# Seven block products in place of eight in the second layer of a fused attention and two-layer kernel

## The chip, the cores and the metric

The kernel runs on one core of a Trainium2 chip. The core has TensorE (PE in the profile; PEld is its loading of weights), VectorE (DVE), ScalarE (ACT), GpSimd (POOL) and SyncE (SP), which run side by side, each through its own instructions in a fixed order, and wait for each other at semaphores. PE reads SBUF and writes PSUM. The metric is the time of one execution on the device in microseconds (us), as the median of several runs.

## The reference

Attention with a mask by hashes is followed by two layers on 1536 tokens. The change touches the second layer alone (`_moe2_ref`), which has 512 inputs, 1536 hidden features and 512 outputs:

```python
def _moe2_ref(x, w_gate, w_val, w_out):
    gate = 1.0 / (1.0 + np.exp(-(x @ w_gate)))
    val = x @ w_val
    return (gate * val @ w_out).astype(np.float32)
```

## The kernel before

All products are made in three terms: an operand is split into a high part (rounded to the type fp32r, by ScalarE) and a low part (source minus high part, by GpSimd or VectorE), and `three` adds high x high, low x high and high x low into one PSUM tile. A 512-row contraction is thus 4 (`kc`) x 3 matmuls.

The tokens are cut into three sweeps of 512 (`CH`). In the second layer a sweep runs over 12 f-tiles of 128 hidden features. `tiles` lists all (layer, sweep, f-tile) in order; the last 24 entries are the second and the third sweep of the second layer, f-tiles 0 to 11 twice. For each tile the loop in `moe` does the following:

- `weights` splits the tile's piece of w_gate and of w_val (`wah`, `wal`, `wbh`, `wbl`; low parts on GpSimd, line 699).
- `stage1` makes the two first products, gate into the PSUM tile `pa`, value into `pb`, 12 matmuls of 512 token columns each.
- `post` takes the sigmoid of `pa` (ScalarE, `a`), multiplies it into `pb` (VectorE, line 745) and splits that into `gh` (ScalarE) and `gl` (VectorE, line 748).
- `second`, one tile behind, multiplies `gh` and `gl` with the split piece of w_out (`wth`, and `wtl` by VectorE at line 699) and adds into four PSUM tiles `m0` to `m3`, 12 matmuls of 512 columns. After the last f-tile of a sweep the four are copied out and stored.

The raw weights come from memory as 64-bit numbers and are decoded (`decode`) into SBUF, where all of them stay; decoding ends in the first sweep of the second layer. In this last stage the order on each engine is set by a list scheduler that works from its own estimates of durations; the source gives it priorities by the place in the program.

Of the kernel before, what the change touches and what calls it, by code (L numbers as in the profile page):

```python
# [229 lines left out]
def lsh_attention_moe_moe2_kernel(  # L230
# [380 lines left out]
    def open_mw():  # L611
        mw = Tiles(ctx.enter_context(tc.tile_pool(name="mw", bufs=1, side="left", reuse_waits="tile")), "mw", 1)
        late["mw"] = mw
        for nm in ("w1", "w2"):
            late[nm] = [mw.tile([P, KC, P], F32, name=f"{nm}r{i}") for i in range(NF1)]
        late["xh"] = mw.tile([P, KC, CH], F32R, name="xh")
        late["xl"] = mw.tile([P, KC, CH], F32R, name="xl")
# [102 lines left out]
    def moe(psM):  # L720


        tiles = [(1, s, fi) for s in range(1, NSW) for fi in range(NF1)] + [(2, s, fi) for s in range(NSW) for fi in range(NF2)]
        mp, mw = late["mp"], late["mw"]
        x2 = [(late["xh"], late["xl"])]
        x2 += [[mp.tile([P, KC, CH], F32R, name=f"x2_{i}_{t}") for i in range(2)] for t in range(1, NSW)]
        split_x(1, x2[1], range(KC))

        def weights(n):

            if n >= len(tiles):
                return None
            m, s, fi = tiles[n]
            ga, gb = (late["w1"][fi], late["w2"][fi]) if m == 1 else ftile(fi)[:2]
            return [split_w(mp, "wa", ga), split_w(mp, "wb", gb)]

        def post(n, ps):
            m, s, fi = tiles[n]
            a = mp.tile([P, CH], F32, tag="a", name="a", bufs=2)
            if m == 1:  # L740
                act_copy(a, ps[0])
            else:
                act.activation(out=a, in_=ps[0], func=AF.Sigmoid)
# [7 lines left out]
        def second(n, g, wt, acc):  # L751
            m, s, fi = tiles[n]
            nf = NF1 if m == 1 else NF2
            last = n == len(tiles) - 1
            mm = None
            for c in range(4):
                cs = slice(c * P, (c + 1) * P)
                with tc.issue_after(mm.ins) if last and c else nullcontext():
                    if m == 1:
                        mm = three(acc[c], [t[:, cs] for t in wt], g, fi == 0, fi == nf - 1)  # L760
                    else:
                        mm = three(acc[c], [t[:, cs] for t in g], wt, fi == 0, fi == nf - 1)
            if fi < nf - 1:
                return
            for c in range(4):
                if m == 1:
                    act_copy(x2[s][0][:, c], acc[c])
                    dve.tensor_tensor(out=x2[s][1][:, c], in0=acc[c], in1=f(x2[s][0][:, c]), op=ALU.subtract)
                else:
                    o = mp.tile([P, DM], F32, tag="a" if last and c < 2 else "o", name="o", bufs=2)  # L770
                    if last and c % 2:
                        dve.tensor_copy(o, acc[c])
                    else:
                        act_copy(o, acc[c])
                    b, n = divmod(s * (CH // P) + c, NT)
                    sync.dma_start(out=out[b * S:(b + 1) * S].rearrange("(p c) d -> c p d", c=NT)[n], in_=o)

        ops = {0: weights(0), 1: weights(1)}
        gs, wts = {}, {}
        acc = None  # L780
        for n in range(len(tiles) + 1):
            if n < len(tiles):
                ps = [psM.tile([P, 512], F32, tag=t, name=t) for t in ("pa", "pb")]
                x = x2[tiles[n][1]]
                w = ops.pop(n)
                for kcs in ([range(KC)] if n else [range(KC - 1), range(KC - 1, KC)]):
                    for i in range(2):
                        stage1(ps[i], w[i], x, kcs)
                m, s, fi = tiles[n]
                wts[n] = split_w(mp, "wt", wc[:, fi] if m == 1 else ftile(fi)[2], eng=dve)  # L790
                gs[n] = post(n, ps)
# [5 lines left out]
            second(n - 1, gs.pop(n - 1), wts.pop(n - 1), acc)  # L797
# [3 lines left out]
            if n + 1 < len(tiles):  # L801
                ops[n + 1] = weights(n + 1)
            if n == 3:
                split_x(2, x2[2], range(KC))

    def decodes(n):

# [127 lines left out]
```

## Time and profile before

| | |
|---|---|
| median of 3 runs | 826.63 us (825.66 to 826.91) |
| profiled execution | 824.83 us |
| its span, first to last instruction | 823.0 us |
| PE busy | 795.7 us, 97% of the span |
| DVE, ACT, POOL busy | 523.7, 511.1, 347.6 us |
| mean granted clock of PE | 1.00 |

The span is what the rows are measured in; the execution's own time has 1.8 us around it. A row of the trace names the engine, the line of the kernel, the operation and its tiles (out<-in). The duration of an instruction reaches from its start to its modelled end, and the next of the same engine can start before that.

### The profile page before, as it was taken

The page shows a single profiled execution, that of the slowest core. Times are in us where ns is not written, and L with a number is a line of the kernel's source. Part 1 is how long each engine was busy: PE and PEld are TensorE (multiplying, and loading weights), DVE is VectorE, ACT ScalarE, POOL GpSimd, SP SyncE. Part 2 cuts the span into 40 slices and gives each one's busy share as a digit, 9 for nine tenths or more (in the row PEclk, how much of TensorE's full clock was granted, in tenths as well). Part 3 has the DMA queues.
Part 4 walks back from the last instruction along what each step waited for, and adds up shares of the span by engine and source line. Part 5 has one row for each costly group of instructions (what it writes and reads, how often), then busy time and mean ns, then how long its engine had stood idle before and what let it go on. Part 6 is the DMA issues. An engine that isn't in the chain of part 4 may idle for free.

```text
span 823.0 us, 11970 instructions
## 1 busy us (share of the span) xinstructions
PE 795.7 (97%) x4144; PEld 667.9 (81%) x4144; DVE 523.7 (64%) x929; ACT 511.1 (62%) x993; POOL 347.6 (42%) x360
## 2 busy tenths in 40 slices
PE   6898999999999999999999999999999999999998
PEld 4676888888788888888888888888888888888886
DVE  7869989888799989988175545686642222322222
ACT  6888878776788888777355555755634333343332
POOL 4566443133565464349333434444533333333330
PEclk9999999999999999999999999999999999999999
DMA  7865645344354544330013122343301000010001
GB/s 234 211 200 171 187 115 158 98 122 122 96 155 132 148 129 115 101 111 13 1 53 101 53 77 77 103 129 127 103 1 52 0 1 1 0 52 1 0 1 52
DMA packets 45949, 74.11 MB, mean 90 GB/s; under 512 B 6336, under 2 KB 32960, under 8 KB 45888
## 3 DMA queue, kind: packets, MB, share of 16 engines
q1 hardware_dynamic: 45888, 73.34, 30.5%
q8 instruction: 33, 0.54, 0.3%
q14 instruction: 28, 0.23, 0.1%
HBM read 52.43 MB, written 3.19 MB: 68 GB/s over the span
## 4 chain that ended last, share of the span: by engine, by line
PE 83%; DVE 9%; ACT 2%; DMA 2%; POOL 2%; issue 1%; SPq 0%; POOLq 0%; DVEq 0%; ACTq 0%
PE pa L705 17%; PE m L705 17%; PE pb L705 17%; PE av L541 7%; PE tp L523 5%; PE wacc L600 4%; PE p L705 4%; PE s L469 3%; PE s L472 3%; DVE s L479 3%; PE y L705 2%; PE gps L402 2%; DVE pt L528 2%; DVE da L338 1%; PE trr L394 1%
## 5 line engine op out<-in xcount | busy, mean ns | idle before, releaser
L745 DVE TENSOR_TENSOR pb<-pb,a 128x512 f32<-128x512 f32 x52 | 36.3, 698 | 147.7 <-PE pb L705 140.4
L523 PE MATMUL tp<-idf,e 128*128 128x128 f32 x576 | 102.4, 275 | 5.8 <-DVE pt L528 5.4
L490 ACT ACTIVATE e<-s,sm 128x768 f32<-128x768 f32 x96 | 95.8, 1000 | 15.7 <-DVE sm L480 14.9
L526 ACT ACTIVATE pt<-tp 128x384 fp32r<-128x384 f32 (+1 forms) x192 | 89.9, 493 | 19.8 <-PE tp L523 17.4
L705 PE MATMUL pa<-x,wah 128*128 128x512 f32 x320 | 98.7, 389 | 0.0
L336 POOL TENSOR_SCALAR da<-da 128x512 f32<-128x512 f32 x76 | 52.7, 695 | 108.9 <-ACT da L334 104.4
L479 DVE TENSOR_REDUCE s<-s 128x1 f32<-128x768 f32 x96 | 91.1, 954 | 11.6 <-PE s L472 10.4
L705 PE MATMUL pb<-x,wbh 128*128 128x512 f32 x320 | 98.5, 389 | 0.0
L699 POOL TENSOR_TENSOR wal<-xall,wah 128x512 fp32r<-128x512 f32 x36 | 47.4, 1316 | 110.1 <-ACT wah L277 109.6
L528 DVE TENSOR_TENSOR pt<-tp,pt 128x384 fp32r<-128x384 f32 x168 | 87.8, 547 | 4.1 <-ACT pt L526 2.9
L523 PEld LDWEIGHTS tp<-idf,e 128*128 128x128 f32 x576 | 71.3, 140 | 19.6 <-DVE pt L528 6.8
L541 PE MATMUL av<-pt,spv 128*128 128x256 f32 (+1 forms) x576 | 85.1, 297 | 1.7 <-DVE pt L528 1.4
L541 PEld LDWEIGHTS av<-pt,spv 128*128 128x128 f32 (+1 forms) x576 | 72.6, 182 | 11.1 <-DVE pt L528 2.4
L334 ACT ACTIVATE da<-st 128x512 f32<-128x512 f32 x76 | 51.0, 671 | 48.6 <-DVE w1r L343 20.6
L705 PEld LDWEIGHTS pb<-x,wbh 128*128 128x128 f32 x320 | 60.1, 188 | 12.5
L705 PEld LDWEIGHTS pa<-x,wah 128*128 128x128 f32 x320 | 60.1, 188 | 12.5
L469 PE MATMUL s<-bk,bq 128*128 128x384 f32 x192 | 61.9, 384 | 6.3 <-ACT e L490 6.0
L600 PE MATMUL wacc<-wo,t 128*128 128x512 f32 x192 | 64.1, 416 | 1.7 <-DVE pt L528 1.6
L705 PE MATMUL pb<-x,wbl 128*128 128x512 f32 x160 | 62.3, 389 | 0.0
L705 PE MATMUL pa<-x,wal 128*128 128x512 f32 x160 | 62.2, 390 | 0.0
L748 DVE TENSOR_TENSOR gl<-pb,gh 128x512 fp32r<-128x512 f32 x52 | 35.9, 690 | 39.8 <-ACT gh L277 39.8
L338 DVE SCALAR_TENSOR_TENSOR da<-st,da 128x512 uint32<-128x512 uint32 x76 | 58.5, 771 | 1.2
(143 smaller groups left out, 1856.6 us busy)
## 6 DMA issues: line engine op xcount, KB each, us to landing
st<-in_moe_w_dram SPq DMA_DIRECT2D x32, 512.0 KB, 4.1
st<-in_moe_w_out_dram SPq DMA_DIRECT2D x20, 512.0 KB, 3.7
st<-in_moe_w_gate_dram SPq DMA_DIRECT2D x12, 512.0 KB, 3.5
st<-in_moe_w_val_dram SPq DMA_DIRECT2D x12, 512.0 KB, 3.5
rawq<-in_q_dram SPq DMA_DIRECT2D x16, 192.0 KB, 3.4
rawk<-in_k_dram SPq DMA_DIRECT2D x16, 192.0 KB, 4.1
rr<-row SPq DMA_DIRECT2D x16, 192.0 KB, 3.2
out_dram<-o SPq DMA_DIRECT2D x12, 256.0 KB, 2.1
```

The source lines that it names most:

```text
L334: act.activation(out=f(a), in_=f(hw), func=AF.Abs)
L336: pool.tensor_scalar(out=f(a), in0=f(a), scalar1=F64_HI, scalar2=F64_LO, op0=ALU.min, op1=ALU.max)
L338: dve.scalar_tensor_tensor(out=a, in0=hw, scalar=0xC0000000, in1=a, op0=ALU.bitwise_and, op1=ALU.bitwise_or)
L469: pe.matmul(s[:, half, :HS], lhsT=m["bq"][:, qs], rhs=m["bk"][:, ks], start=True, stop=False)
L479: dve.tensor_reduce(out=one[:, 1:2], in_=s[:, :, :HS], op=ALU.max, axis=AX.XY, negate=True)
L490: act.activation(out=e.rearrange("p (a c) -> p a c", a=2), in_=s[:, :, :HS], func=AF.Exp, bias=sm[:, 1:2], scale=sm[:, 0:1], accum_out=su_ ...
L523: pe.transpose(ps[:, j * P:(j + 1) * P], e[:, c * P:(c + 1) * P], idf)
L526: act.activation(out=dh, in_=src, func=AF.Copy)
L528: dve.tensor_tensor(out=d, in0=src, in1=f(dh), op=ALU.subtract)
L541: pe.matmul(acc[:w.shape[1], :2 * P].rearrange("p (a t) -> p a t", a=2), lhsT=w, rhs=r[:, :, c], start=(c == 0 and i == 0), stop=(c == NT ...
L600: pe.matmul(acc, lhsT=t3[x][:, j], rhs=wo[y][:, j], start=(j == 0 and n == 0), stop=(j == NF1 - 1 and n == 2))
L705: mm = pe.matmul(ps, lhsT=lhs[x], rhs=rhs[y], start=start and n == 0, stop=stop and n == 2)
```

## The change

For the second and third sweep two f-tiles are now taken together (`pairs`, 12 of them). The product of the 512 x 256 weights of a pair with 512 x 512 tokens is cut into blocks: the weights into contraction halves x f-tiles, the tokens into contraction halves x token halves. Seven products of blocks (Strassen's scheme in Winograd's form) replace eight, for the gate and for the value (`k` in 0, 1). A block product has 2 x 3 matmuls of 256 token columns.

- `blocks` makes four sums of token blocks once a sweep (eight operations of VectorE on 512 columns) and splits them: `S` keeps three, the fourth overwrites a block of the tokens.
- `t1`, `t24`, `t3` make the differences of weight blocks (VectorE, eight of 256 columns a pair); `t24`, `t3`, `t1low` and `own` split them (ScalarE and GpSimd). They are issued for the next pair during a pair.
- `product` writes into one half of a PSUM tile, in the order 1, 6, 2, 7, 4, 5, 3, each for gate and value; four halves for each of the two are used in turn.
- Each product is added to the running results in SBUF: `A` for the gates, `vs` for the values (14 additions of 256 columns by VectorE, one operand in PSUM, and two copies by ScalarE). Sigmoid, gate product (lines 945 and 965 of the changed kernel), `gh` and `gl` (line 922) follow in SBUF, where before they read PSUM.
- The second products of the pair before, eight groups of three matmuls, are issued between the block products.

```diff
+        def blocks(s, tmp):
...
+            t1, t2, t3, t4 = (t.rearrange("p (k f) -> p k f", k=2) for t in tmp)
+            add(t1, *A[1, 0])
+            add(t2, *A[1, 1])
+            add(t2, t2, t1)
+            add(t3, *A[0, 0])
+            add(t1, t3, t1, ALU.subtract)
+            add(t3, t2, t3, ALU.subtract)
+            add(t4, *A[0, 1])
+            add(t4, t4, t3, ALU.subtract)
+            low(dve, *A[1, 0], t4)
+            return {1: A[0, 0], 2: A[0, 1], 3: A[1, 0], 4: A[1, 1]}, {5: t2, 6: t3, 7: t1}
...
+            def t24(p, k):
+
+                if p < len(pairs):
+                    _, _, b21, b22 = raw(p, k)
+                    h, l = h24[(2 * p + k) % 3]
+                    r = r24[k]
+                    sub(r[:, :2 * P], b22, r1[:, k * 2 * P:(k + 1) * 2 * P])
+                    sub(r[:, 2 * P:], b21, r[:, :2 * P])
+                    low(pool, h, l, r)
+                    W[p % 2][k, 6], W[p % 2][k, 4] = [[half(t, i) for t in (h, l)] for i in range(2)]
+
+            def t3(p, k):
+
+                if p < len(pairs):
+                    _, b12, _, b22 = raw(p, k)
+                    h, l = hb3[(2 * p + k) % 3]
+                    r = r3[:, k * 2 * P:(k + 1) * 2 * P]
+                    sub(r, b22, b12)
+                    low(pool, h[:, :2 * P], l[:, :2 * P], r)
+                    low(pool, h[:, 2 * P:], l[:, 2 * P:], b22)
...
+            def product(p, k, i):
+
+                q = (7 * p + place[i]) % 4
+                r = banks[k][q % 2][:, q // 2 * 2 * P:(q // 2 + 1) * 2 * P]
+                w, x = W[p % 2][k, i], X[i]
+                for kk in range(2):
+                    three(r, [t[:, kk] for t in w], [t[:, kk] for t in x], kk == 0, kk == 1)
+                return r
...
+            for p, (s, n) in enumerate(pairs):
+                if p == NS:
+                    X = {**nextX, **S}
+                elif p == NS - 2:
+                    nextX, nextS = blocks(2, [xf[0][:, 3], xf[1][:, 3]] + [mp.tile([P, CH], F32, tag="o", name="tmp", bufs=2) for _ in range(2)])
...
+                def gate(i):
+                    gh = mw.tile([P, CH], F32R, tag="gh0", name="gh", bufs=2)
+                    gl = mw.tile([P, CH], F32R, tag="gl0", name="gl", bufs=2)
+                    act_copy(gh, vs[i])
+                    dve.tensor_tensor(out=gl, in0=vs[i], in1=f(gh), op=ALU.subtract)
+                    gs[n + i] = gh, gl
+
+                for k in range(2):
+                    act_copy(C[k][0][:, hi2], product(p, k, 1))
+                for k in range(2):
+                    add(C[k][1][:, lo2], product(p, k, 6), C[k][0][:, hi2])
+                renew(6)
+                sec()
...
+                for k in range(2):
+                    add(C[k][0][:, hi2], product(p, k, 4), C[k][1][:, hi2])
+                    if k == 0:
+                        act.activation(out=A[0], in_=A[0], func=AF.Sigmoid)
+                dve.tensor_tensor(out=vs[0], in0=vs[0], in1=A[0], op=ALU.mult)
+                gate(0)
+                own(p + 1, 1)
+                t1(p + 1)
+                t24(p + 1, 0)
+                sec()
+                wts[n] = split_w(mp, "wt", ftile(tiles[n][2])[2], eng=dve)
+                sec()
+                for k in range(2):
+                    r = product(p, k, 5)
+                    add(C[k][1][:, hi2], r, C[k][1][:, hi2])
+                    add(C[k][1][:, lo2], r, C[k][1][:, lo2])
+                renew(5)
+                t3(p + 1, 0)
+                sec()
...
+            if n == N - 3:
+                seven = sevens()
+                next(seven)
...
+        for _ in seven:
+            pass
```

Where the scheduler puts this is seen in the order of the instructions. On VectorE, near the end of the first sweep, the last decoding (lines 338 and 343) is followed by the post of a tile and the low part of its w_out:

```order
L343 ISA wc<-da,dr 128x1024
L338 SCALAR_TENSOR_TENSOR da<-st,da 128x512
L343 ISA wc<-da,dr 128x1024
L745 TENSOR_TENSOR pb<-pb,a 128x512
L748 TENSOR_TENSOR gl<-pb,gh 128x512
L699 TENSOR_TENSOR wtl<-wc,wth 128x512
```

In the changed kernel the same place reads as follows (line 787 are the sums of token blocks, x_0_1 and x_1_1 the high and the low tokens of the second sweep, line 778 the low parts of the sums):

```order
L338 SCALAR_TENSOR_TENSOR da<-st,da 128x512
L787 TENSOR_TENSOR tmp<-x_0_1_5060,x_1_1_5061 128x512 x2
L343 ISA wc<-da,dr 128x1024
L787 TENSOR_TENSOR tmp<-tmp 128x512
L787 TENSOR_TENSOR tmp<-x_0_1_5060,x_1_1_5061 128x512 x2
L745 TENSOR_TENSOR pb<-pb,a 128x512
L787 TENSOR_TENSOR tmp<-tmp 128x512 x2
L748 TENSOR_TENSOR gl<-pb,gh 128x512
L778 TENSOR_TENSOR st_6938<-tmp,st_6938 128x512
L787 TENSOR_TENSOR tmp<-tmp 128x512
L778 TENSOR_TENSOR st_6936<-tmp,st_6936 128x512
```

The eight sums and two of the four low parts stand around and between the rows of that post; its `wtl` comes behind them.

On VectorE at the first pair of the second sweep, the changed kernel has these rows (line 828 are the differences of weights, line 882 the additions of products to the results; x_0_2 and x_1_2 are the tokens of the third sweep):

```order
L787 TENSOR_TENSOR xlf<-x_0_2_5062,x_1_2_5063 128x512
L745 TENSOR_TENSOR pb<-pb,a 128x512
L828 TENSOR_TENSOR xhf<-xall 128x256
L828 TENSOR_TENSOR xhf<-w1r_2782,w1r_2781 128x256
L787 TENSOR_TENSOR xhf<-x_0_2_5062,x_1_2_5063 128x512
L828 TENSOR_TENSOR xlf<-w1r_2779,xlf 128x256
L828 TENSOR_TENSOR xlf<-xall 128x256
L828 TENSOR_TENSOR xlf<-xall,xhf 128x256
L748 TENSOR_TENSOR gl<-pb,gh 128x512
L699 TENSOR_TENSOR wtl<-w2r_2787,wth 128x512
L787 TENSOR_TENSOR xlf<-xlf,xhf 128x512
L828 TENSOR_TENSOR xlf<-w1r_2782 128x256
```

Before, the post of a tile (745, 748) and `wtl` (699) were alone there; now sums for the third sweep and differences for the first and the second pair stand between its rows. The first addition of a product (882) comes two rows later.

On GpSimd a tile of these sweeps has one `wal` and one `wbl` (line 699) before, four operations of 512 columns for two tiles. A pair in the middle of the second sweep has these rows after (line 778 the low parts of differences and sums, `wl` two of 512, `dr` four of 256, `st_6939` one of 512):

```order
L778 TENSOR_TENSOR wl<-xlf,wh 128x512
L699 TENSOR_TENSOR wal<-xall,wah 128x512
L699 TENSOR_TENSOR wbl<-w1r_2779,wbh 128x512
L778 TENSOR_TENSOR dr<-xlf,da 128x256 x2
L778 TENSOR_TENSOR wl<-xlf,wh 128x512
L778 TENSOR_TENSOR st_6939<-xhf,st_6939 128x512
L778 TENSOR_TENSOR dr<-wc,da 128x256
L778 TENSOR_TENSOR dr<-xall,da 128x256
```

Two of the four `wal` and `wbl` went, and seven operations came.

## Rows read from the trace of the kernel before

**Rows 1.** the page's part 1: busy us, share of the span, instructions

```profile
PE 795.7 (97%) x4144; PEld 667.9 (81%) x4144; DVE 523.7 (64%) x929; ACT 511.1 (62%) x993; POOL 347.6 (42%) x360
```

**Rows 2.** the chain that ended last: start us, length us, what it ran

```profile
620.54 2.72 PE pa L705 x12
...
808.22 2.72 PE pa L705 x12
...
813.66 5.45 PE m L705 x24
...
819.14 0.69 DVE o L772
```

**Rows 3.** busy us of each engine in three stretches

```profile
core 0: us, PE busy (x) PEld busy (x) DVE busy (x) ACT busy (x) POOL busy (x), PEclk, DMA share, GB/s
200.00:300.00 100.00, 95.10 (x618) 82.71 (x617) 90.49 (x174) 83.31 (x177) 53.73 (x59) 1.00 0.47 129
600.00:620.00 20.00, 20.00 (x90) 16.57 (x89) 7.99 (x11) 7.19 (x12) 7.48 (x6) 1.00 0.01 1
680.00:800.00 120.00, 120.00 (x531) 99.39 (x530) 30.55 (x44) 46.24 (x78) 38.77 (x30) 1.00 0.03 9
```

**Rows 4.** timeline of PE in attention; then line 541's duration, minimum, median, maximum

```profile
205.72 1.59 PE L541 MATMUL av<-pt,spv 128*128 128x256 f32 x12
...
214.73 1.65 PE L541 MATMUL av<-pt,spv 128*128 128x256 f32 x12
...
L541 PE MATMUL av<-pt,spv x171: 275/280/386, 199.7 to 300.0; 128*128 128x256 f32 x171
```

**Rows 5.** groups of VectorE, 620 to 820; the last of the whole span

```profile
L748 DVE TENSOR_TENSOR gl<-pb,gh 128x512 fp32r<-128x512 f32 x24 | 16.6, 691 | 16.7 <-ACT gh L277 16.7
L699 DVE TENSOR_TENSOR wtl<-w2r,wth 128x512 fp32r<-128x512 f32 x16 | 11.1, 692 | 20.3 <-ACT wth L277 20.3
...
L554 DVE TENSOR_TENSOR xall<-av,xall 64x256 f32<-64x256 f32 x42 | 17.4, 414 | 6.7 <-ACT xall L277 6.1
```

**Rows 6.** a group of GpSimd, 620 to 820; and tile spv (minimum, median, maximum)

```profile
L699 POOL TENSOR_TENSOR wal<-xall,wah 128x512 fp32r<-128x512 f32 x22 | 28.4, 1290 | 90.9 <-ACT wah L277 90.9
...
L383 POOL TENSOR_TENSOR spv<-rawv,spv x14: 1004/1016/1481, 46.4 to 337.8; 128x384 fp32r<-128x384 f32 x14
```

**Rows 7.** groups of ScalarE, 620 to 820; the last of the whole span

```profile
L277 ACT ACTIVATE wah<-xall 128x512 fp32r<-128x512 f32 x22 | 13.9, 632 | 37.7 <-PE pa L705 37.7
...
L277 ACT ACTIVATE xall<-av 64x256 f32<-64x256 f32 x48 | 18.2, 380 | 10.8 <-PE av L541 9.9
```

**Rows 8.** timeline of VectorE and of GpSimd in three places: start us, us

```profile
533.58 0.68 DVE L338 SCALAR_TENSOR_TENSOR da<-st,da 128x512 uint32<-128x512 uint32 x1
534.18 1.78 DVE L699 TENSOR_TENSOR wtl<-w2r,wth 128x512 fp32r<-128x512 f32 x1
...
534.09 1.32 POOL L699 TENSOR_TENSOR wal<-xall,wah 128x512 fp32r<-128x512 f32 x1 [2.72 <-ACT wah L277]
...
700.88 0.69 DVE L748 TENSOR_TENSOR gl<-pb,gh 128x512 fp32r<-128x512 f32 x1 [0.66 <-ACT gh L277]
...
700.00 1.29 POOL L699 TENSOR_TENSOR wbl<-wc,wbh 128x512 fp32r<-128x512 f32 x1 [1.43 <-ACT wbh L277]
...
376.28 3.50 DVE L699 TENSOR_TENSOR wtl<-wc,wth 128x512 fp32r<-128x512 f32 x2
...
373.97 1.83 POOL L699 TENSOR_TENSOR wal<-w1r,wah 128x512 fp32r<-128x512 f32 x1 [1.67 <-ACT wah L277]
...
379.20 1.74 POOL L699 TENSOR_TENSOR wbl<-w2r,wbh 128x512 fp32r<-128x512 f32 x1
```

**Rows 9.** tiles gl and wtl: durations ns minimum, median, maximum

```profile
L748 DVE TENSOR_TENSOR gl<-pb,gh x52: 680/691/693, 413.9 to 815.1; 128x512 fp32r<-128x512 f32 x52
...
L699 DVE TENSOR_TENSOR wtl<-wc,wth x28: 681/691/1786, 376.3 to 809.0; 128x512 fp32r<-128x512 f32 x28
```

**Rows 10.** TensorE's waits: us in total, times, longest us

```profile
PE s L469 <- ACT e L490: 6.0, 6, 1.6
```

More of the change, by code (lines that the diff above doesn't have):

```diff
@@ L615, in open_mw @@
             late[nm] = [mw.tile([P, KC, P], F32, name=f"{nm}r{i}") for i in range(NF1)]
-        late["xh"] = mw.tile([P, KC, CH], F32R, name="xh")
-        late["xl"] = mw.tile([P, KC, CH], F32R, name="xl")
+        late["xh"] = mw.tile([P, KC, CH], F32R, tag="xh", name="xh")
+        late["xl"] = mw.tile([P, KC, CH], F32R, tag="xl", name="xl")
         for i in range(NF1):
@@ L749, in post, with second @@
             return gh, gl
-        def second(n, g, wt, acc):
+        def second(n, c):
             m, s, fi = tiles[n]
@@ L754, in second @@
             last = n == len(tiles) - 1
[L755 to L764, printed above, removed]
@@ L765, in second @@
-            for c in range(4):
+            cs = slice(c * P, (c + 1) * P)
+            g, wt = gs[n], wts[n]
+            with tc.issue_after(late["mm"]) if last and c else nullcontext():
                 if m == 1:
-                    act_copy(x2[s][0][:, c], acc[c])
-                    dve.tensor_tensor(out=x2[s][1][:, c], in0=acc[c], in1=f(x2[s][0][:, c]), op=ALU.subtract)
-                else:
[L770 to L776, printed above, removed]
+                    mm = three(acc[c], [t[:, cs] for t in wt], g, fi == 0, fi == nf - 1)
+                else:
+                    mm = three(acc[c], [t[:, cs] for t in g], wt, fi == 0, fi == nf - 1)
@@ new lines, in second @@
+            late["mm"] = mm.ins
+            if fi == nf - 1 and m == 1:
+                act_copy(x2[s][0][:, c], acc[c])
+                dve.tensor_tensor(out=x2[s][1][:, c], in0=acc[c], in1=f(x2[s][0][:, c]), op=ALU.subtract)
+            elif fi == nf - 1:
+                o = mp.tile([P, DM], F32, tag="a" if last and c < 2 else "o", name="o", bufs=2)
+                if last and c % 2:
+                    dve.tensor_copy(o, acc[c])
+                else:
+                    act_copy(o, acc[c])
+                b, n = divmod(s * (CH // P) + c, NT)
+                sync.dma_start(out=out[b * S:(b + 1) * S].rearrange("(p c) d -> c p d", c=NT)[n], in_=o)
@@ new lines, in low, with add @@
+        def low(eng, hi, lo, src):
+            act_copy(hi, src)
+            eng.tensor_tensor(out=lo, in0=src, in1=f(hi), op=ALU.subtract)
+        def blocks(s, tmp):
+            A = {(i, j): [t[:, 2 * j:2 * j + 2, i * CH // 2:(i + 1) * CH // 2] for t in x2[s]] for i in range(2) for j in range(2)}
+            def add(o, a, b, op=ALU.add):
+                dve.tensor_tensor(out=o, in0=f(a), in1=f(b), op=op)
+            t1, t2, t3, t4 = (t.rearrange("p (k f) -> p k f", k=2) for t in tmp)
[9 more added lines that the diff above has]
+            return {1: A[0, 0], 2: A[0, 1], 3: A[1, 0], 4: A[1, 1]}, {5: t2, 6: t3, 7: t1}
@@ L780, in moe @@
         acc = None
[L781 to L791, printed above, removed]
+        N = NF1 * (NSW - 1) + NF2
+        for n in range(N):
+            ps = [psM.tile([P, 512], F32, tag=t, name=t) for t in ("pa", "pb")]
+            x = x2[tiles[n][1]]
+            w = ops.pop(n)
+            for kcs in ([range(KC)] if n else [range(KC - 1), range(KC - 1, KC)]):
+                for i in range(2):
+                    stage1(ps[i], w[i], x, kcs)
+            m, s, fi = tiles[n]
+            wts[n] = split_w(mp, "wt", wc[:, fi] if m == 1 else ftile(fi)[2], eng=dve)
+            gs[n] = post(n, ps)
             if n == 0:
@@ L796, in moe @@
                        psT.tile([P, 512], F32, tag="t", name="m2"), psT.tile([P, 512], F32, tag="t", name="m3")]
-            second(n - 1, gs.pop(n - 1), wts.pop(n - 1), acc)
+            for c in range(4):
+                second(n - 1, c)
             with tc.issue_after(late["gl"]):
@@ L800, in moe @@
                     decode()
-            if n + 1 < len(tiles):
+            if n + 1 < N:
                 ops[n + 1] = weights(n + 1)
+            if n == N - 3:
+                seven = sevens()
+                next(seven)
             if n == 3:
                 split_x(2, x2[2], range(KC))
+        for _ in seven:
+            pass
     def decodes(n):
```

92 lines of the change are left out of this document (added).

## Prediction

> **What bounds the kernel now.** I read the page's table of busy time first [rows 1]: TensorE (PE) is busy 97% of the span. The chain of waits over the layer that changes says what that means [rows 2]: from 620.54 us to 819.1 us it holds PE alone, in runs of twelve matmuls that take 2.72 us, so one 128x512 matmul per 2.72/12 = 0.2267 us and nothing between them. A tile is three runs (gate, value, second product), 8.16 us; 620.54 to 808.22 is 23 of them, so the 24 tiles of the second and third sweep fill 620.54 to 816.4. The granted clock is 1.00 in every stretch [rows 3], TensorE's higher level of 2.4 GHz. The other engines have room in those sweeps: in 680 to 800 VectorE (DVE) works 30.6 us of 120, ScalarE (ACT) 46.2, GpSimd (POOL) 38.8 [rows 3]. So fewer PE cycles are a gain one for one, for as long as the others, which take on the work of Strassen's sums, stay ahead of PE.
>
> **What PE saves.** A pair of tiles now has 2 x 36 = 72 matmuls of 512 columns: 72 x 0.2267 = 16.32 us. After, the second products stay (24 of 512), and 7 block products x 2 matrices x 2 k-halves x 3 terms = 84 matmuls of 256 columns replace 48 of 512. The layer has no 256-column matmul now, but attention has: runs of 12 last 1.59 to 1.65 us, one alone 0.28 [rows 4], so (1.59 - 0.28)/11 = 0.119 us from one to the next, at worst (1.65 - 0.28)/11 = 0.1245. That is over half of 0.2267: of the eighth that Strassen saves in columns, part goes to the fixed cost of a matmul. Pair: 24 x 0.2267 + 84 x 0.119 = 15.44 us, 0.88 us less; twelve pairs: **-10.6 us** (with 0.1245: -5.1). I take 0.119, since the row of 1.65 may hold a wait.
>
> The Trainium skill ("TensorE: Matmul & The Clock Gate", Back-to-back issue gap) gives N/2.4 + 2.5 ns for an isolated matmul: 215.8 ns for 512 columns, 109.2 for 256. By it the saving would be 48 x 0.2158 - 84 x 0.1092 = 1.19 us a pair, 14.2 in all; the row of 0.2267 is 11 ns above it, and the row decides.
>
> **What the others get.** From the loop's body, for a pair: DVE does 14 additions of 256 columns with one operand in PSUM, and, with both operands in SBUF, 8 differences of weights of 256 columns and 6 operations of 512 (two gate products, two gl, two wtl). Before, a pair had 6 of 512 in all, and four of these read PSUM. A 512 takes 0.69 us [rows 5] and the next starts 0.08 before its end (533.58 + 0.68 against 534.18, [rows 8]): 0.61. For 256 columns the nearest row is 64x256, 0.414 us [rows 5], so 0.33. DVE per pair: 6 x 0.61 + 22 x 0.33 = 10.9 us, where it had 3.7. POOL has five low halves of 512 at 1.29 [rows 6], and four of 256; by the 384-column row (1.004 at least) these are 1.29 - 2 x 0.286 = 0.72: 9.3 us, where it had 5.2. ACT has 2 copies and 4 high halves of 256 (0.38 [rows 7]) and 7 high halves, 2 sigmoids and 2 gh of 512 (0.63 at most): 9.2 us. All are below 15.44, and by busy time alone the change would give its 10.6 us.
>
> **Why I don't believe that.** In before, DVE and POOL get in each other's way, and only for one kind of operation. gl<-pb,gh, with one operand in PSUM, never takes over 0.693 us in 52 executions [rows 9], also where POOL works through it (700.88 beside POOL's 700.00, [rows 8]). wtl, with both in SBUF, has the same median and a maximum of 1.786 [rows 9]. At 534.18 it starts 0.09 us after POOL's 1.32 us operation and ends 1.78 later, 0.55 after POOL's end (535.41): it did nothing until POOL was through, then its 0.55. POOL in turn ended 1.15 after DVE's earlier operation ended (534.26). From 373.97 to 381.0 both had work queued: POOL's four operations took 1.74 to 1.83 each in place of 1.29, and DVE's two wtl 3.50 in place of 1.38 [rows 8]. So an operation of POOL and a two-SBUF operation of DVE exclude each other; POOL holds 1.15 us, DVE 0.55 (for 256 columns half of each, 0.57 and 0.27, an estimate by columns). The Trainium skill says the same, and of a whole instruction ("SBUF — State Buffer", Who interferes with whom); it speaks against the change, since 14 DVE operations a pair are now of that kind, against 2.
>
> Per pair POOL holds 5 x 1.15 + 4 x 0.57 = 8.0 us and DVE 6 x 0.55 + 8 x 0.27 = 5.5: 13.5 of 15.4 us, by two queues in order. A DVE operation of the kind finds POOL inside with a chance of 8.0/15.4 = 0.52 and waits about half a hold, 0.5: 14 x 0.52 x 0.5 = 3.7 us. DVE then needs 14.6 us a pair. Between the bounds, no block (10.9) and every hold of POOL blocks (18.9), I take 14.6: it just fits, with 0.8 to spare, so what comes on top is late, and PE waits for it:
> - Preparation. The eight sums of blocks(1) and their four low parts are 12 operations of 512, 7.3 us, and the first pair's differences 2.6; with 20 x 0.52 x 0.5 of blocks 15.1. DVE idles some 12 of the 19 us ahead of 620.5 (7.99 busy in 600 to 620, [rows 3]): 3.1 late. The order puts the eight sums for the third sweep here too, three ahead of the first addition of a product and nearly all the others before the second pair ends: 8 x (0.61 + 0.26) = 7.0, against 2 x 0.8 spare. 3.1 + 7.0 - 1.6 = 8.5 us late. Some 6 us of leeway stand against it, as products 1, 6 and 2 and their second products need none of this: 2.5 to 8.5. Since the additions that free PSUM stand behind the sums in DVE's order, the leeway helps little: I take **7.5**.
> - The turn to the third sweep: four low parts, 4 x 0.87 = 3.5, less 0.8: **2.7**.
> - The other nine pairs and the tail: what stands behind a blocked operation is an addition that frees a PSUM half, and PE waits for that half four products later. Between nothing and one full hold a pair (1.1), half: **5.0**.
>
> Waits: 15.2 us (bounds 2.5 and 21.1). I count no loss of clock with them: attention's waits of up to 1.6 us [rows 10] left the granted clock at 1.00 in 200 to 300 [rows 3]. The end is as before: 24 second products (5.45 us, [rows 2]), of which the first twelve cover the last gate.
>
> **The sum.** The profiled execution takes 824.83 us (span 823.0 and 1.8 around it); 824.83 - 10.6 + 15.2 = 829.4. The median of the runs is 1.8 above the profiled one: **831.2 us**, 0.6% slower.
>
> **Rivals.**
> - The blocks hide: DVE has idle time between additions, and POOL's work falls beside the 14 PSUM additions (4.6 us a pair). For it: in the steady sweeps of before no wtl was blocked (mean 0.692, [rows 5]); against it: there POOL had a third of the time, now 60%. With waits of 2 us at most: 826.6 - 10.6 + 2 = 818. It decides if waits stay below 9.
> - It cancels: waits of 9 to 12.3 us, 825.0 to 828.3.
> - The pair becomes DVE-bound: if POOL blocks 5.8 us a pair, halfway to all, DVE needs 16.7 us, more than the 16.32 of before; 826.6 + 12 x 0.4 + 10.2 for preparation and turn = 842. It decides from 4.5 us of blocks a pair. For it: alternation at 373.97 to 381.0; against it: POOL is idle 6 us a pair and waits for ACT.
> - The saving is smaller: matmuls at 0.1245 give 5.1 in place of 10.6; with the waits 836.7, without them 821.5. That the products aren't saved can't be: the order shows 84 matmuls a pair.
>
> **Chances.** Forecast 0.50 (its own range 828.5 to 836.7), hidden 0.20, cancels 0.13, DVE-bound or fewer PE savings 0.17. A measurement here tells 0.2%, 1.65 us, from no change. Faster: the hidden case and a little of the small-waits edge, 0.22; same 0.13; slower 0.65. The range, 818 to 842, leaves out part of the hidden and of the DVE-bound case.
>
> **What would show it.** Right: 256-column matmuls 0.119 us apart; DVE's L828, L787, L945 and L922 with means well above 0.41 and 0.69 while L882, with a PSUM operand, has 0.41; PE idle for DVE, some 15 us in all, most of it in the first three pairs and at the turn; steady pairs of about 15.4 us. Wrong: two-SBUF means near their free times, or PE without waits, which would make it the hidden case; or a matmul spacing of 0.125 or more.

## The result, and the profile after

The changed kernel takes 833.68 us (median, 833.31 to 834.98), beside 826.25 us of the kernel before on the same chip: a ratio of 1.010 (95% interval 1.0087 to 1.0112), 0.9 to 1.1% slower. 831.2 was forecast. The profiled execution took 834.98 us, span 833.2, and is the slowest of the four. In it TensorE ran at 1.2 GHz twice before the end, from 16.07 to 19.48 us, in attention, which the change doesn't touch, and from 726.04 to 729.45. Its mean granted clock is 0.995; the other three have 0.997 to 0.998, which leaves room for one such stretch and not for both. Which of the two they lack can't be told.

The page's table of busy time, against [rows 1]:

```profile
PE 795.7 (96%) x4576; PEld 684.3 (82%) x4576; DVE 669.3 (80%) x1217; ACT 546.3 (66%) x1085; POOL 414.7 (50%) x420
```

VectorE works 146 us more, TensorE as long as before in a longer span: its busy time holds the low clock and what it loses behind each wait, so that the saving doesn't show in it. Where TensorE stands still is seen in stretches of the second and third sweep (core 0, columns as in [rows 3]; 620 to 651 is the first pair and most of the second, which ends at 658; the turn to the third sweep lies in 713 to 733):

```profile
620.00:651.00 31.00, 26.24 (x169) 22.89 (x168) 30.90 (x52) 16.15 (x33) 21.11 (x17) 1.00 0.09 35
698.00:713.00 15.00, 15.00 (x105) 13.98 (x105) 13.13 (x26) 7.39 (x16) 9.64 (x9) 1.00 0.00 0
713.00:726.00 13.00, 10.46 (x76) 9.75 (x75) 11.56 (x21) 7.95 (x17) 11.40 (x9) 1.00 0.00 1
726.00:729.40 3.40, 3.40 (x13) 2.82 (x12) 3.40 (x9) 1.02 (x2) 0.00 (x0) 0.51 0.00 0
791.00:806.00 15.00, 15.00 (x105) 14.00 (x104) 11.85 (x26) 7.02 (x15) 6.68 (x6) 1.00 0.01 1
```

In the first row VectorE (third busy figure) has 0.1 us left of 31 and TensorE is short of 4.8. In the fourth row the granted clock is 0.51. The waits of TensorE from 600 us on (for whom: us in total, times, longest):

```profile
PE pa L705 <- DVE a L882: 3.9, 3, 2.5
PE m L705 <- ACT gh L277: 2.9, 4, 1.6
PE pb L705 <- DVE a L882: 1.9, 2, 1.6
PE pa L705 <- DVE xhf L882: 1.3, 3, 0.6
PE pb L705 <- DVE xhf L882: 0.6, 2, 0.5
```

All but one are waits for VectorE's additions (L882) to free PSUM, or for a `gh` whose gate product stands behind them in VectorE's order. The exception is the first and longest wait for `gh`, at the start: it belongs to the last tile of the old form, whose gate product (L745) stood behind differences of weights and a sum for the third sweep:

```profile
620.17 1.52 DVE L828 TENSOR_TENSOR xlf<-w1r,tmp 128x256 f32<-128x256 f32 x1
621.61 0.95 DVE L828 TENSOR_TENSOR xlf<-w1r 128x256 f32<-128x256 f32 x1
622.48 1.22 DVE L787 TENSOR_TENSOR xlf<-x,x 128x512 f32<-128x512 f32 x1
623.63 0.69 DVE L745 TENSOR_TENSOR pb<-pb,a 128x512 f32<-128x512 f32 x1
...
625.00 0.50 PE L705 MATMUL m<-wth,gh 128*128 128x512 f32 x1 [1.62 <-ACT gh L277]
```

The additions themselves are not slow. Groups from 600 us on, to be read beside [rows 5, 6]:

```profile
L882 DVE TENSOR_TENSOR a<-pa,a 128x256 f32<-128x256 f32 x42 | 17.0, 414 | 4.2 <-PE pa L705 4.1
L699 DVE TENSOR_TENSOR wtl<-w2r,wth 128x512 fp32r<-128x512 f32 x16 | 16.2, 1014 | 1.9 <-ACT wth L277 1.9
L945 DVE TENSOR_TENSOR xhf<-xhf,a 128x512 f32<-128x512 f32 x12 | 10.7, 892 | 0.4
L828 DVE TENSOR_TENSOR xlf<-xall 128x256 f32<-128x256 f32 x12 | 9.5, 794 | 0.3 <-POOL dr L778 0.3
L828 DVE TENSOR_TENSOR xlf<-w1r 128x256 f32<-128x256 f32 x8 | 9.4, 1172 | 3.0 <-POOL dr L778 3.0
L778 POOL TENSOR_TENSOR wl<-xlf,wh 128x512 fp32r<-128x512 f32 x23 | 33.4, 1455 | 30.2 <-ACT wh L277 30.2
```

With one operand in PSUM an addition takes 0.414 us in each of its four forms. With both in SBUF the same size takes 0.63 on the mean of all 92 differences: 0.79 and 1.17 in the two groups shown, but 0.41 in groups that stand behind other operations of VectorE. Operations of 512 columns take 0.89 (L945) or 1.01 (`wtl`, 0.692 in [rows 5]), and GpSimd's `wl` 1.455 against 1.290.

The wait at the turn shows the chain. Timelines of VectorE, GpSimd and TensorE (start us, us):

```profile
720.68 1.45 DVE L699 TENSOR_TENSOR wtl<-wc,wth 128x512 fp32r<-128x512 f32 x1
722.05 1.49 DVE L828 TENSOR_TENSOR xlf<-xall 128x256 f32<-128x256 f32 x1
723.47 0.41 DVE L882 TENSOR_TENSOR a<-pa,a 128x256 f32<-128x256 f32 x1
723.80 0.87 DVE L945 TENSOR_TENSOR xhf<-xhf,a 128x512 f32<-128x512 f32 x1
724.60 0.41 DVE L882 TENSOR_TENSOR a<-pa,a 128x256 f32<-128x256 f32 x1
...
720.10 1.48 POOL L778 TENSOR_TENSOR wl<-xlf,wh 128x512 fp32r<-128x512 f32 x1
721.77 1.49 POOL L778 TENSOR_TENSOR st<-xhf,st 128x512 fp32r<-128x512 f32 x1 [0.20 <-ACT st L277]
...
722.24 0.28 PE L705 MATMUL pb<-x,dr 128*128 128x256 f32 x1
725.06 0.51 PE L705 MATMUL pa<-x,wah 128*128 128x256 f32 x2 [2.54 <-DVE a L882]
725.40 0.29 PE L705 MATMUL pa<-x,wal 128*128 128x256 f32 x1
...
726.60 0.63 PE L705 MATMUL m<-wth,gh 128*128 128x512 f32 x1
727.03 0.63 PE L705 MATMUL m<-wtl,gh 128*128 128x512 f32 x1
```

`xlf` starts 0.28 us after GpSimd's `st` and ends at 723.54, 0.28 after GpSimd's end (723.26): it did nothing until GpSimd was through. The additions behind it are late, and TensorE starts 0.05 us after the second of them ended (725.01). From 726 on its matmuls of 512 columns are 0.43 us apart, not 0.23.

For all runs below I add up TensorE's **lost time**: the sum, over all distances between two matmul starts after 600 us, of what they have beyond 0.2268 us (512 columns) or 0.1202 (256), the distances where nothing waits. It is -0.1, so nothing, in before and 18.9 us here. By place (distances over 0.025 us late): 8.8 in the first two pairs, 1.9 in the next three, 4.4 at the turn, 3.5 behind it, of which 0.7 come in the last second products. 2.5 of it is a second cost of the waits, 24 times 0.10 us: the second matmul behind a wait comes late too (725.40 - 725.06 = 0.34 for two, not 0.24). 1.5 is the low clock at the turn.

### The profile page after: what moved, and what is told of

It reads as the page before. It is cut to its first block, busy times and chain, and to the rows that moved or that the text cites. A ratio compares the mean times of both kernels' runs of the same rounds, so it can differ in the third digit from the quotient of the medians.

```text
span 833.2 us, 13347 instructions
## 1 busy us (share of the span) xinstructions
PE 795.7 (96%) x4576; PEld 684.3 (82%) x4576; DVE 669.3 (80%) x1217; ACT 546.3 (66%) x1085; POOL 414.7 (50%) x420
## 4 chain that ended last, share of the span: by engine, by line
PE 60%; DVE 22%; ACT 6%; issue 6%; DMA 3%; POOL 2%; SPq 0%; ACTq 0%; DVEq 0%; POOLq 0%
PE m L705 11%; PE pa L705 10%; PE pb L705 10%; PE av L541 7%; PE tp L523 4%; PE wacc L600 4%; PE p L705 4%; DVE s L479 3%; PE s L469 3%; PE s L472 2%; PE y L705 2%; DVE pt L528 2%; DVE da L338 2%; DVE xlf L828 2%; PE gps L402 2%
## 5 line engine op out<-in xcount | busy, mean ns | idle before, releaser
L490 ACT ACTIVATE e<-s,sm 128x768 f32<-128x768 f32 x96 | 95.7, 999 | 15.9 <-DVE sm L480 15.4
L705 PE MATMUL m<-wth,gh 128*128 128x512 f32 x144 | 57.4, 399 | 3.0 <-ACT gh L277 2.9
L705 PE MATMUL m<-wtl,gh 128*128 128x512 f32 x144 | 57.1, 396 | 0.0
L472 PE MATMUL s<-ak,aq 128*128 128x384 f32 x192 | 56.5, 360 | 0.0
L705 PE MATMUL pa<-x,wah 128*128 128x512 f32 (+1 forms) x176 | 48.9, 361 | 3.1 <-DVE a L882 3.1
L335 ACT ACTIVATE dr<-st 128x512 int32<-128x512 uint32 x76 | 50.7, 668 | 0.0
L705 PE MATMUL pb<-x,wbh 128*128 128x512 f32 (+1 forms) x176 | 48.5, 360 | 0.0
L778 POOL TENSOR_TENSOR wl<-xlf,wh 128x512 fp32r<-128x512 f32 x23 | 33.4, 1455 | 30.2 <-ACT wh L277 30.2
L705 PE MATMUL m<-wth,gl 128*128 128x512 f32 x144 | 48.5, 394 | 0.0
L745 DVE TENSOR_TENSOR pb<-pb,a 128x512 f32<-128x512 f32 x28 | 19.5, 695 | 35.5 <-PE pb L705 28.2
```

What stands on the lines that cost most here:

```text
L472: pe.matmul(s[:, half, :HS], lhsT=m["aq"][:, qs], rhs=m["ak"][:, ks], start=False, stop=True)
L490: act.activation(out=e.rearrange("p (a c) -> p a c", a=2), in_=s[:, :, :HS], func=AF.Exp, bias=sm[:, 1:2], scale=sm[:, 0:1], accum_out=su_ ...
```

## The experiments

At these distances a pair of seven products saves 16.32 - (84 x 0.1202 + 24 x 0.2268) = 0.78 us. So each run can be checked against a sum: before, less 0.78 a pair, plus the lost time of its own trace.

| run | pairs | lost time, us | sum, us | measured, us | ratio to before (95%) |
|---|---|---|---|---|---|
| changed kernel | 12 | 18.9 | 835.8 | 833.7 | 1.0087 to 1.0112 |
| GpSimd writes zeros | 12 | 1.5 | 818.0 | 817.5 | 0.9882 to 0.9915 |
| GpSimd, one operand, once | 12 | 3.0 | 819.6 | 819.2 | 0.9902 to 0.9932 |
| GpSimd, one operand, twice | 12 | 7.7 | 824.3 | 824.2 | 0.9966 to 0.9985 |
| zeros for two of nine | 12 | 9.3 | 825.9 | 825.4 | 0.9988 to 1.0007 |
| sums of the third sweep later | 12 | 18.2 | 834.7 | 834.4 | 1.009 to 1.0123 |
| gate and value in one bank | 12 | 17.0 | 833.6 | 833.1 | 1.0071 to 1.0099 |
| third sweep alone | 6 | 3.8 | 825.1 | 825.0 | 0.9986 to 1.0003 |
| third sweep, one bank | 6 | 0.3 | 821.6 | 821.3 | 0.9933 to 0.9957 |
| from third pair, one bank (early overwrite) | 10 | 2.0 | 820.0 | 819.7 | 0.9916 to 0.994 |
| from fourth pair, one bank (early overwrite) | 9 | 1.0 | 819.8 | 820.7 | 0.9923 to 0.995 |
| from third pair, one bank, mended | 10 | 1.5 | 819.7 | 819.4 | 0.9907 to 0.9935 |
| from fourth pair, one bank, mended | 9 | 1.0 | 820.0 | 819.8 | 0.9914 to 0.9942 |

Apart from the changed kernel, whose profiled execution was its slowest, sums and times agree within 0.9 us, most within 0.5. In the two runs marked "early overwrite" some products read changed tokens, as told below.

**GpSimd out of SBUF's reads.** Theory A is the prediction's: GpSimd's operations and VectorE's two-SBUF operations exclude each other. Rival B: VectorE simply has too much to do.

```diff
-            eng.tensor_tensor(out=lo, in0=src, in1=f(hi), op=ALU.subtract)
+            if eng is pool:
+                pool.memset(f(lo), 0.0)
+            else:
+                eng.tensor_tensor(out=lo, in0=src, in1=f(hi), op=ALU.subtract)
```

(and the same in `split_w` for `own`.)

> In the pairs of seven products GpSimd writes zeros into the low halves of the weights in place of source minus high part, with the same tiles in the same places of its order: it reads nothing of SBUF there (the low parts of these weights are left out of the result). Everything on the other engines stays. Theory A (operations of GpSimd that read two SBUF operands and two-SBUF operations of VectorE exclude each other): VectorE's means at L828, L945, L965 and wtl come back from 0.75 to 1.17, 0.89, 0.76 and 1.01 us to about 0.41 and 0.69; TensorE's waits in the pairs fall from 18.6 us to 0 to 5; 826.3 - 10.6 + 0 to 5 = 816 to 821 us. Rival B (VectorE's own 10.9 us a pair, its order and the depth of PSUM make TensorE wait, whatever GpSimd does): the means may fall, but the waits stay at 15 or more and the time at 831 to 834.

Measured: 817.5 us, lost time 1.5. Groups of VectorE from 600 us on (L888, L951, L834 are L882, L945, L828 of the changed kernel), and 620 to 806 us, first of the changed kernel, then of this one:

```profile
L888 DVE TENSOR_TENSOR a<-pa,a 128x256 f32<-128x256 f32 x42 | 17.1, 420 | 5.8 <-PE pa L708 4.9 <-ACT wth L277 0.5
L702 DVE TENSOR_TENSOR wtl<-w2r,wth 128x512 fp32r<-128x512 f32 x16 | 11.0, 685 | 2.2 <-ACT wth L277 2.0
L951 DVE TENSOR_TENSOR xhf<-xhf,a 128x512 f32<-128x512 f32 x12 | 8.3, 688 | 0.6
L834 DVE TENSOR_TENSOR xlf<-xall 128x256 f32<-128x256 f32 x12 | 5.0, 418 | 2.3 <-PE pb L708 2.3
L834 DVE TENSOR_TENSOR xlf<-w1r 128x256 f32<-128x256 f32 x8 | 3.3, 416 | 0.0
```

```profile
620.00:806.00 186.00, 175.13 (x1171) 159.53 (x1170) 166.29 (x318) 99.52 (x197) 117.47 (x99) 0.99 0.03 12
```

```profile
620.00:806.00 186.00, 185.82 (x1290) 173.26 (x1288) 141.73 (x338) 104.12 (x204) 40.42 (x94) 1.00 0.04 13
```

Every two-SBUF group of the pairs is back at 0.42 and 0.69 us, VectorE does 20 operations more in 24.6 us less, and TensorE has no wait worth a row. A holds, B falls. One thing changed beside: zeros don't wait for ScalarE's high half, so GpSimd is also earlier. Operation by operation the traces tell the two apart. From 650 us on, 33 two-SBUF operations of VectorE lie over one of GpSimd's writes by 0.1 us or more, and none takes over 0.43 us (256 columns) or 0.70 (512). In the changed kernel 58 lie so over one of GpSimd's subtractions and take 1.04 and 1.08 us on the mean, while the 107 additions with an operand in PSUM that do so take 0.43 at most. The Trainium skill ("SBUF — State Buffer", Who interferes with whom) says of a two-SBUF operation of VectorE that it contends with a GpSimd instruction that reads SBUF, and not with one that only writes it; the 0.42 us beside GpSimd's 40.4 us of zeros agree.

**One operand, once and twice.** Does it take two operands on GpSimd's side?

```diff
+            if eng is pool:
+                pool.tensor_scalar(out=lo, in0=src, scalar1=0.0, scalar2=0.0, op0=ALU.mult, op1=ALU.add)
```

(the second run has this line twice.)

> As with the zeros, but GpSimd works through the high part's source once (source times 0 plus 0, one operand in SBUF), so it reads half of what the subtraction reads; the low parts of these weights are left out again, and the result is the one of the zeros. If it is enough for the exclusion that GpSimd reads SBUF at all, VectorE's two-SBUF operations stay longer than 0.41 and 0.69 us while GpSimd is inside, and the time lies between the two, 820 to 830 us; if two operands on both sides are wanted, it is as with the zeros, 816 to 821. Rival B again: 831 to 834.

> GpSimd does its pass over one operand twice for each low half (2 x 0.73 us for 512 columns), so that it works as long as with the subtraction, but reads one operand of SBUF at a time; the low parts of these weights are left out, as with the single pass. If GpSimd's time inside an operation is what keeps VectorE out, the waits come back: 829 to 834 us. If what counts is that the subtraction reads two operands, VectorE gets in beside or between the passes: 818 to 824 us.

Measured: 819.2 and 824.2 us. Timelines of the single pass, VectorE and GpSimd:

```profile
649.53 0.41 DVE L834 TENSOR_TENSOR xlf<-xall 128x256 f32<-128x256 f32 x1
649.86 1.12 DVE L951 TENSOR_TENSOR xhf<-xhf,a 128x512 f32<-128x512 f32 x1
...
649.82 0.62 POOL L782 TENSOR_SCALAR st<-xhf 128x512 fp32r<-128x512 f32 x1 [0.39 <-PE pa L708]
650.47 0.78 POOL L782 TENSOR_SCALAR dr<-xall 128x256 fp32r<-128x256 f32 x1
```

VectorE's gate product (0.69 us alone) starts 0.04 after GpSimd's pass and ends 0.54 after its end (650.44): it was kept out by an operation that reads one operand. GpSimd's next, 0.41 us when free, then took 0.78. So one operand is enough, though the times lie where two operands had been said to be wanted (the second 0.2 us beyond). What makes them short may be the length of one hold: with two passes GpSimd is busier than in the changed kernel (126.4 us from 620 to 806, against 117.5), and TensorE loses 7.7 us, not 18.9:

```profile
620.00:806.00 186.00, 182.26 (x1244) 167.65 (x1243) 159.04 (x331) 105.91 (x204) 126.43 (x202) 1.00 0.04 13
```

The same time in holds of about half the length would keep VectorE waiting about half as long at each meeting. That is argued and not shown; the passes also start without ScalarE's high half, and the two were not told apart.

**A dose.** Zeros for `wal` and `wbl` alone.

```diff
-                    hl = split_w(mp, ("wa", "wb")[k], ftile(tiles[pairs[p][1]][2])[k])
+                    hl = split_w(mp, ("wa", "wb")[k], ftile(tiles[pairs[p][1]][2])[k], eng=None)
```

(with `eng=None` it writes zeros.)

> Zeros only for the low parts of the undifferenced weights (wal, wbl, two of GpSimd's nine operations a pair; these low parts are left out of the result); the other seven subtract as before. This is a dose: GpSimd's hold falls from 5 x 1.15 + 4 x 0.57 = 8.0 us a pair to 5.7. Theory A: blocks and waits fall by 0.3 or more, from 18.6 to 9 to 13 us: 825 to 829 us. Rival B: no change, 831 to 834.

Measured: 825.4 us, lost time 9.3. Two of nine operations, 29% of GpSimd's hold, carry half of the loss (1.5 us of it the low clock at the turn, which this trace doesn't have). So the loss is no fixed price for each operation; that it is what no longer fits is the reading, not a measurement.

**Sums later.** The prediction blamed the third sweep's sums, which stand at the start, for most of the loss there.

```diff
                 elif p == NS - 2:
+                  with tc.issue_after(late["gl"]):
                     nextX, nextS = blocks(2, [xf[0][:, 3], xf[1][:, 3]] + [mp.tile([P, CH], F32, tag="o", name="tmp", bufs=2) for _ in range(2)])
```

> The eight sums of tokens for the third sweep, which the order puts ahead of and among the first pairs of the second, are held until the gl of pair 3; nothing else changes and the result is the same. If their place made the first three pairs wait (10 of the 18.6 us of waits lie in the first two pairs and the start), the start's waits fall to about 4 and 1 to 2 come back later: 826 to 829 us. Rival: VectorE is late at the start anyway by the second sweep's own sums and differences, or the same waits come up in pairs 3 to 6: 831 to 834.

Measured: 834.4 us, the rival's range. The first two pairs lose 6.0 in place of 8.8, and 1.5 of the 6.0 is a low clock from 635.2 on that the changed kernel doesn't have there; so the waits at the start did fall to about 4.5, as expected. But 7.3 are lost at 688 to 713, where the sums now stand (0.8 in the changed kernel), and not 1 to 2. Most of that stretch:

```profile
698.00:713.00 15.00, 10.76 (x71) 9.21 (x70) 15.00 (x23) 5.40 (x11) 10.72 (x9) 1.00 0.00 0
```

VectorE is busy for all of it and TensorE short of 4.2 us. Neither of the two places tried in the sweep of seven products has room for the eight operations of 512 columns; moving them moved the wait.

**PSUM's depth.** Each PSUM tile of 512 columns, a bank in what follows, holds two products in its halves. In the changed kernel these are two gate products or two value products; a half comes up again after four products, its bank after two. At the turn TensorE's product 1 waited for the second addition of product 5, which by the rotation is in the other half of the same tile; its own half was last read two products earlier. In the changed kernel's trace none of the 168 additions that read such a half overlaps a write to the other half, with products and halves taken from the order of the code.

```diff
-                r = banks[k][q % 2][:, q // 2 * 2 * P:(q // 2 + 1) * 2 * P]
+                r = banks[q // 2][q % 2][:, k * 2 * P:(k + 1) * 2 * P]
...
+                rs = [product(p, k, 6) for k in range(2)]
                 for k in range(2):
-                    add(C[k][1][:, lo2], product(p, k, 6), C[k][0][:, hi2])
+                    add(C[k][1][:, lo2], rs[k], C[k][0][:, hi2])
```

(and so for the other six products.)

> All as in the changed kernel, but a product's gate and value share a bank of PSUM, one half each, and the two gate and value products are issued ahead of the two additions; the four banks then hold four products, so that TensorE's next write to a bank waits for the additions four products back, where in the changed kernel it waited for those two back. The result is the same. Theory P (depth: TensorE waits because a bank's other half is still being read): waits fall from 18.6 us to 12 or less, 825 to 828 us. Rival (VectorE as a whole is late, and depth only moves a wait): 831 to 834. I hold the rival for likelier, since VectorE was busy 15.9 of 16 and 15.0 of 15 us in the two pairs that waited most.

Measured: 833.1 us, lost time 17.0, the rival. Three stretches:

```profile
620.00:651.00 31.00, 26.71 (x176) 24.50 (x175) 29.35 (x51) 16.01 (x34) 21.44 (x17) 0.94 0.10 35
651.00:667.00 16.00, 12.92 (x75) 11.56 (x74) 15.86 (x28) 6.42 (x13) 9.66 (x8) 0.89 0.01 2
744.00:806.00 62.00, 62.00 (x432) 57.95 (x431) 52.43 (x114) 33.45 (x70) 39.32 (x35) 1.00 0.04 15
```

Where VectorE is late as a whole (start, turn) the waits come later and longer, and three times the clock falls with them, which costs 4.7 of the 17.0 us. Without the low clock the start loses 8.8 and 8.9 us in the two mappings, and the turn 2.9 and 2.4; but the pairs between and behind lose 0.6 where the changed kernel loses 5.4. So by the time the rival holds, and by the waits theory P is half right: they fall from 17.4 to 12.3 us, and the low clock takes most of that back. Behind the turn the new mapping, with its order of issue, was all that was wanting.

**The third sweep alone,** in both mappings: `pairs` over `range(2, NSW)`, `blocks(2)` in place of `blocks(1)`, no turn.

```diff
-            pairs = [... for s in range(1, NSW) for i in range(NS)]
+            pairs = [... for s in range(2, NSW) for i in range(NS)]
...
-        N = NF1 * (NSW - 1) + NF2
+        N = NF1 * (NSW - 1) + 2 * NF2
```

> Seven products in the third sweep alone; the second sweep keeps its tiles of eight products, and there is no turn. The result is the same. TensorE saves 6 x 0.88 = 5.3 us. In the changed kernel the third sweep had 3.5 us of waits behind the turn, and the sums and first differences now stand in a sweep in which VectorE works a quarter of the time. If waits come where VectorE and GpSimd together have more than fits: 2 to 5 us of waits, 823 to 826 us, faster than before or the same. Rival: the start costs what it cost in the second sweep (8.8 us in the first two pairs) wherever it stands: 829 to 831 us.

> Both: seven products in the third sweep alone, and gate and value of a product in one bank. The result is the same. By theory P the steady pairs lose their waits as well, where VectorE has its work done in time on the whole: 0.5 to 2 us of waits, 821 to 823.5 us. If depth does nothing: as with the third sweep alone, 823 to 826.

Measured: 825.0 and 821.3 us. The first can't be told from before; the second is 0.4 to 0.7% faster. 729 to 806 us, first in the changed kernel's mapping, then with gate and value in one bank:

```profile
729.00:806.00 77.00, 74.84 (x517) 69.45 (x516) 64.25 (x128) 39.63 (x77) 42.91 (x38) 1.00 0.02 8
```

```profile
729.00:806.00 77.00, 77.00 (x539) 71.87 (x539) 63.12 (x132) 37.63 (x77) 41.74 (x36) 1.00 0.02 8
```

VectorE's and GpSimd's work is the same within 2 us; with four products between a write and the additions it must wait for, the lateness of single operations is absorbed and TensorE never waits. (The issue order changed with the mapping, both products ahead of both additions, and the two were not told apart.) And the first two pairs, which lost 8.8 us behind decoding, lose 1.4 behind tiles of eight products, and 0.1 with one bank: preparation costs little where VectorE has room. Here no sums for a further sweep stand beside it; the next runs have them.

**Later in the second sweep.** So: one bank, and the second sweep's first four (or six) f-tiles as eight products.

```diff
-            pairs = [... for s in range(1, NSW) for i in range(NS)]
+            pairs = [... for s in range(1, NSW) for i in range(2 if s == 1 else 0, NS)]
+            NS -= 2
...
-        N = NF1 * (NSW - 1) + NF2
+        N = NF1 * (NSW - 1) + NF2 + 4
```

> Seven products with gate and value of a product in one bank, but the second sweep does its first four f-tiles as eight products and takes seven from its third pair on: ten pairs in all, 10 x 0.88 = 8.8 us saved. The preparation then stands in tiles of the old form, when decoding is over and VectorE works some 4 of 16 us. The result is the same. If the start waits only because the preparation meets decoding and the first pair: no waits at the start, the turn's 3.8 us (of which 1.7 are TensorE at 1.2 GHz) stay, and 825.9 - 8.8 + 4 = 821 us, with up to 2 more if the sums for the third sweep come too close: 820 to 823. Rival: the second sweep waits at its start wherever that is (7 to 12 us): 827 to 829.

> The same from the second sweep's fourth pair on: nine pairs, 9 x 0.88 = 7.9 us saved, one more pair of the old form ahead; the sums for the third sweep stand in the second of its three pairs in the second sweep. The result is the same. If preparation costs nothing in tiles of the old form and the turn costs 3.8 us: 825.9 - 7.9 + 4 = 822 us (820.5 to 823.5), about the ten pairs' time. Rival: sums and turn crowd three pairs, 6 us or more of waits: 824 to 826.

Measured: 819.7 and 820.7 us. In both, the fourth sum overwrites a block of the second sweep's tokens while tiles of eight products still read it, so that these read changed tokens and the output is not the layer's; the work for the engines is the same. Mended, that low half is made behind the last such tile:

```diff
+            if s > 1:
                 low(dve, *A[1, 0], t4)
...
             X.update(S)
             yield
+            low(dve, *X[3], todo[3])
```

> Ten pairs from the second sweep's third pair on, as in the run of ten pairs before, but the block of tokens that its fourth sum replaces is overwritten only when the last tile of eight products has read it, which in that run was too early; that low half now stands at the first pair. The run of ten pairs had 2.0 us of waits and took 819.7 us. If that one operation, 0.7 us on VectorE, and GpSimd's first low halves behind it, still come in time for product 7 (fourth of the pair, some 4.4 us after its start): 819 to 821 us. If they don't: 1 to 3 us of waits at the first pair, 821 to 823.

> The same with nine pairs; the run of nine pairs had 1.0 us of waits and took 820.7 us. In time: 820 to 822 us, and behind the ten pairs by the 0.88 us of one pair. Late: 822 to 824.

Measured: 819.4 us (ten pairs, 0.6 to 0.9% faster than before) and 819.8 (nine), the two shortest times of a kernel that computes the whole layer. All of TensorE's waits from 600 us on, ten pairs:

```profile
PE m L705 <- DVE gl L925: 0.5, 2, 0.3
```

The sums for the third sweep all stand between 619.0 and 646.3 us here, in tiles of eight products, ahead of the first block product (653.7), and the start and the turn, with its four low parts, lose 0.6 us together. Which of the two is better can't be told: 819.0 to 820.2 and 819.2 to 821.0.

## Why the prediction came out

**What held.** The main step did: two-SBUF operations of VectorE wait for GpSimd, the lateness reaches TensorE through the additions, and the saving is eaten. L828, L945 and `wtl` are longer, as foretold, and L882 is untouched. Zeros on GpSimd give back 17.4 of 18.9 us of lost time and 16.2 us of time. The end is as before: 3.9 us from the last matmul's end to the end of the span in both (819.1 of 823.0, 829.3 of 833.2); only the second products ahead of it lose 0.7 us to late `gh` and `gl`.

**PE's saving, -10.6.** A block product's matmuls are 0.120 us apart (twelve in 1.44 us), not 0.119, and where nothing waits pairs follow each other in 15.59 us (third sweep alone, one bank: block products at 748.12, 763.71, 779.30 and 794.88), not 15.44. The saving is 9.4 by the distances, 8.8 by the pairs; 1 to 2 us too much was forecast.

**Waits, +15.2.** 18.9 in the profiled execution; by the medians 7.4 + 9.4 = 16.8. Parts: start and preparation 8.8 (7.5 forecast), turn 4.4 (2.7), the rest 5.4 (5.0). Two things in the 18.9 had not been counted, the 0.10 us behind the waits (2.5) and the low clock (1.5); without them it is 14.9. So the forecast was 2.5 us low: 1.2 in the saving and 1.6 in the waits, less 0.4 because before takes 826.25 us here and not 826.63.

**Steps that were wrong under a right total.**
- "PE waits for that half four products later": it waits for the bank, two products back. Another mapping, with another order of issue, removed 3.5 us of waits in six pairs. The Trainium skill ("PSUM — Partial Sum Buffer", PSUM bank collisions raise a hardware error) says that the compiler's scheduler orders any two instructions of different engines on one bank and quadrant, other columns included; the trace's 0 of 168 overlaps agree, and no run here shows what an overlap would do.
- "3.7 us" of blocks a pair, and "it just fits, with 0.8 to spare": group by group, and for the same number of operations, the differences, gate products, `gl` and `wtl` of the changed kernel took 35 us longer than with zeros, 2.9 for each pair. Where nothing waits, a pair leaves VectorE more room than 0.8: in the third sweep alone, with one bank, it works 63.12 of 77.00 us (the row of 729 to 806 above), some 13 of 15.6 us a pair.
- "Half: 5.0" for the other pairs: the 5.4 measured came from the depth of two products, not from a pair that just fits; with four, and the other order of issue, they lose 0.6. That the middle between two bounds lay near it is luck.
- "The order puts the eight sums for the third sweep here too", 7.0 us of lateness, against 3.1 for the preparation: held back, the sums took some 4 us from the start, and as much was there without them. Within the sweep of seven products their place decides little, since 7.3 were lost where they then stood; ahead of it, in tiles of eight, they cost nothing.
- "I count no loss of clock": 1.5 us at the turn, behind a wait of 2.5. That waits up to 1.6 us had cost nothing in one trace [rows 10] said nothing of longer ones, and little of such waits elsewhere: in the changed kernel's trace the clock fell in attention too, behind a wait of 1.44.

The rivals: the blocks don't hide; it doesn't cancel; pairs are not DVE-bound, since TensorE is full from 698 to 713 and from 791 to 806 us.

## What to carry to other kernels

Before work is moved from TensorE to VectorE, add up VectorE's operations with two SBUF operands and GpSimd's that read SBUF as if they were one engine. Here they came to 13.5 of 15.4 us by the forecast, and that fitted only with four products between a write to PSUM and the additions it waits for, and with the preparation elsewhere. When the sum nears the period, look for an operand that can stay in PSUM, for work of GpSimd that only writes, or do less. Count the depth of PSUM in banks whose readers are through, not in halves. Preparation belongs where the engine that makes it has slack: with gate and value in one bank, starting the new scheme two pairs later turned a loss of 0.9% into a gain of 0.8%, though two pairs' saving was given up.

## What had not been expected of the hardware

- The second matmul behind a wait of TensorE comes 0.10 us late too, 24 times in the changed kernel, 2.5 us.
- TensorE's granted clock fell to 1.2 GHz five times in this layer, each time behind a wait of 1.7 to 2.5 us or in the last 0.1 us of one (at 726.0 in the changed kernel, 635.2 with the sums later, 637.9, 658.4 and 730.1 with gate and value in one bank), and cost some 1.5 us each. The length of one wait doesn't decide it: in the changed kernel two waits of 1.6 us in the first pair left it at 2.4, while at 16.07 us, in attention, it fell behind a wait of 1.44.
- A pass of GpSimd over one SBUF operand (0.62 us) keeps a two-SBUF operation of VectorE out as a subtraction does; one that only writes (33 times over such an operation) doesn't.
